# A planned instruction order for two transformer layers: tables that change along the stream, and 3741 operations moved in the queues

## The chip, the cores and the metric

The kernel runs on one core of a Trainium2 chip. The core has five engines, each with an in-order queue of its own: TensorE (PE, matmuls), VectorE (DVE), ScalarE (ACT), GpSimd (POOL) and SyncE (SP, which here only issues DMA transfers). Engines wait for each other through semaphores. The metric is the device time of one execution in microseconds; the time before is the median of three runs, 1028.55 us (1028.09 to 1029.22).

## The reference

Two layers, with the same weights, over one sequence of 2048 rows of 448 numbers in bfloat16. Each layer is an attention block A with 16 heads of 28 and a gated mixing and MLP block B, both behind a layer norm and with a residual:

```python
def _A_ref(x, wqkv, wo):
    qkv = (x @ wqkv).reshape(B, S, 3, H, Dh)  # transposed to q, k, v: B, H, S, Dh
    scores = jnp.einsum("bhqd,bhkd->bhqk", q, k) * (Dh ** -0.5)
    p = _softmax(scores, axis=-1)
    o = jnp.einsum("bhqk,bhkd->bhqd", p, v)
    return o.transpose(0, 2, 1, 3).reshape(B, S, D) @ wo

def _B_ref(x, w1, w2, w3, w4):
    h = _gelu(_layernorm(x, axis=-1) @ w1)
    # four column groups of h, moved by +1, -1, +2 and -2 rows
    x1 = x + jnp.concatenate([g0, g1, g2, g3], axis=-1) @ w2
    return x1 + _gelu(_layernorm(x1, axis=-1) @ w3) @ w4

x = A_x
x = x + _A_ref(_layernorm(x), A_wqkv, A_wo)
x = x + _B_ref(_layernorm(x), B_w1, B_w2, B_w3, B_w4)
x = x + _A_ref(_layernorm(x), A_wqkv, A_wo)
x = x + _B_ref(_layernorm(x), B_w1, B_w2, B_w3, B_w4)
```

Per layer there are 16 x 2048 x 2048 exponentials of scores. They are the largest single piece of work off TensorE.

## The kernel before, in words

**Tiling.** The 2048 rows are 16 tiles of 128. Queries are handled in five chunks a layer (`CHUNKS`: tiles 0-3, 4-7, 8-11, 12-13, 14-15), heads in four groups g of four heads j, keys in tiles of 128. A *block* is one head's scores of 128 keys against 512 queries (or two key tiles against 256), that is one bank of PSUM; there are 2048 of them. `ORDER` says in which order chunks meet which key tiles, so that layer 2 can start while parts of layer 1 are still unfinished; a chunk that is interrupted spills its partial sums through `uscr`.

**The stream of scores.** `t_scores` takes blocks from the list `stream` and writes them into banks 0 to 2 (even unit numbers u) and 3 to 4 (odd ones); `score_ops` issues their matmuls (L1510). `t_exp` then lets ACT take the exponential of a whole unit, two or three blocks, in one instruction into `PT` (L1748). `t_pv` multiplies the results by the values into bank 5 (L1765). A unit waits until the unit two before it has been read out, and its place in `PT` until the product that used it last is done.

**Blocks for DVE.** Some blocks go to DVE instead, which builds the exponential with five instructions: `d_first` reads the bank into `yd` (L1592), `d_chain` does two steps of a polynomial in `fb` (L1619, L1621), scales it into `PD` (L1623) and puts the exponent's bits in (L1626). Which blocks those are is decided while the plan is made, by the tables `R_RATE` (a block takes the third bank of an even unit, which then has two blocks for ACT) and `D_RATE` (a block takes a spare bank), and by limits such as `DTH`, `DDTH`, `DLO`, `DHI` on DVE's load and on how far ahead the block lies.

**Everything else** is written as Python generators that hand in one operation after another and run beside this stream: the layer norms (L1100, L1101, L1106 to L1115), the projections (`proj`, all column-tiled products being issued at L915 as four matmuls of one operation), the norm of the softmax (`t_norm`), the output projection (`t_outproj`), the two halves of block B (`t_mixA`, `t_mixB` with the first product of the MLP evacuated at L2180 by DVE, or at L2176 by ACT with the gelu in it if the exps are all planned; the gelu of a group of tiles in one ACT instruction at L2202) and `t_w4`, its second product. Each ACT switch between exp and gelu costs a table load before and after.

**Two engines for one operation.** The function `both` plans an operation on POOL with DVE as the other choice. Squares of q and k (`sq`) always go to POOL; `z2` (L2019), `xx` (L2105) and `otn` (L1862) go to whichever is free earlier by the plan.

**Fills.** `Sched.keep_pe_busy` puts matmuls of no use (`filler`, L2248, four matmuls of 256 columns into a dead bank) into TensorE's queue wherever the plan leaves it idle, as far as `TARGET` and `WIN` ask.

**The planner.** `Sched.run` simulates the engines with durations written in the generators and picks the next operation by the time at which it could start and by its priority (`RANK` and others). `DOUBT` and `DOUBT2` add margins for results that come from DMA, POOL, DVE or ACT. What comes out is one list of operations (`Plan.all`), numbered in the order in which they were planned, and a queue for each engine. `Plan.add` works out from what an operation reads and writes which others it has to wait for, so any order of the list that keeps the data right is a valid program.

**A rearranged plan.** `Plan.rearranged(moves, weave)` is in the kernel before but unused, since `WEAVE` is empty. For each pair (a, b) of `moves` it takes operation a out of its engine's queue and puts it back right behind operation b. Then it adds all operations anew: `weave` is a string with one letter for each, t, s, v, g or d for PE, ACT, DVE, POOL or SP, and each letter adds the next operation of that engine's queue. At the end it makes sure that every operation reads what the same operations as before have written.

The queues before hold 9619 operations: 6328 of PE, 884 of ACT (781 of them exps), 1587 of DVE, 458 of POOL and 362 of SP. Of PE's, 1171 are fills. 108 blocks are DVE's.

Of the kernel before, what the change touches and what calls it, by code (L numbers as in the profile page):

```python
# [15 lines left out]
ENGS = ("pe", "act", "dve", "pool", "sp")  # L16


MOVES = ()
WEAVE = ()  # L20

FILL_MORE = ()

# [241 lines left out]
class Sched:  # L265
    LAT = {"pe": 0.23, "act": 0.175, "dve": 0.145, "pool": 0.2, "sp": 0.2}
    OWN = {"pe": 0.0, "act": 0.15, "dve": 0.125, "pool": 0.05, "sp": 0.05}
    DOUBT = {"dma": 0.6, "pool": 0.4, "dve": 0.15, "act": 0.1}
    DOUBT2 = {"dma": 0.0, "pool": 0.0, "dve": 0.0, "act": 0.0, "pe": 0.0}
# [354 lines left out]
RLO = 5  # L624
# [45 lines left out]
FMO = 1.59  # L670
SWT = 0.103
Sched.DOUBT = {'dma': 0.8, 'pool': 0.6, 'dve': 0.05, 'act': 0.05}
Sched.LCRED = 0.3


# [4 lines left out]
def build_kernel(nc, A_x, A_wqkv, A_wo, B_x, B_w1, B_w2, B_w3, B_w4, out, n_layers=2):  # L680
# [85 lines left out]
    with st:  # L766
# [864 lines left out]
        def t_scores():  # L1631
# [38 lines left out]

            ringed = set()
            while True:
                if u == 1:
                    yield ("acq", ["b3"])
                    yield ("acq", ["b4"])
# [433 lines left out]
        def t_mixB(L, ch, tiles, direct, pr):  # L2109
# [12 lines left out]
            if direct:  # L2122
                yield from tr_pe(slots, xt)
                for xs in slots:
                    yield ("rel", xs)
            wide = False
            hname = None
            small = L == 0 and tiles == SMALL
            if small:
                yield ("wait", ("kvfree",))  # L2130
                hb = vaug[:, 9:16, :].rearrange("p a b -> p (a b)").rearrange("p (f w) -> p f w", w=NW)
                hkey = [[("vaug", 9 + k) for k in range(f * NW // 512, (f * NW + NW - 1) // 512 + 1)] for f in range(14)]
            elif direct:
                hb, hkey = PT, [[("pt", f)] for f in range(14)]
            else:
                hname = yield ("acq", ["h2T", "h2W"] if ("xdone", 1) in SC.events else ["h2T"], [("xT", xt)])
                wide = hname == "h2W"
                if wide:
                    hkey = [[("vaug", 9 + f)] if f < 7 else [("kT", g, 2 + f) for g in range(4)] for f in range(14)]
                else:  # L2140
                    hb, hkey = h2T, [[("h2T", f), ("xst",)] for f in range(14)]
# [4 lines left out]
                return vaug[:, 9 + f, 128 * i:128 * i + 128] if f < 7 else kT[:, i, 128 * (2 + f):128 * (3 + f)]  # L2146

            late = []
            soft = TANHW.get((L, tiles[0]), 0) and not direct
            fps = 512 // NW  # L2150
            parts = [list(range(f, min(f + fps, 14))) for f in range(0, 14, fps)]
            if wide:
# [89 lines left out]
        def t_final():  # L2242
            for t in range(NT):
                yield ("wait", ("x2", 1, t))
            yield op("sp", 0.05, lambda e: e.nop(), deps=odmas)
# [44 lines left out]
        SC.spawn(t_extra(0, 16), 3)  # L2290
        SC.spawn(t_extra(1, 9), 3)
        SC.spawn(t_final(), 9)
        est = SC.run()

        def again(fn, k):
            return lambda e: [x for _ in range(k) for x in fn(e)]
# [63 lines left out]
```

## Time and profile before

| | |
|---|---|
| median of three runs | 1028.55 us |
| the profiled execution | 1028.86 us |
| its span, first to last instruction | 1027.1 us |
| busy PE / DVE / ACT / POOL | 973.3 / 823.3 / 980.3 / 293.1 us |
| DMA | 62.73 MB, mean 61 GB/s |

A line of the profile names a group by line of the kernel, engine, operation and tiles (out<-in), with the number of instructions; then busy time and the mean length of one; then the time its engine was idle just before them and what ended that. PE's matmuls overlap, so that means of one are longer than their share of the busy time. PEld is the weight load of a matmul. Releasers are inferred.

### The profile page before, as it was taken

How to read it: one execution, taken by the hardware profiler on the slowest of the kernel's cores; microseconds unless marked ns; L12 is line 12 of the kernel's file. 1: busy time of each engine (PE TensorE's matmuls, PEld its weight loads, DVE VectorE, ACT ScalarE, POOL GpSimd, SP SyncE). 2: the span in 40 equal slices, each digit the busy share in tenths (PEclk: the TensorE clock that was granted, in tenths of full speed). 3: DMA queues.
4: the chain of work that ended last, by engine and by line, in shares of the span. 5: the costliest groups of instructions: out<-in, count | busy, mean ns of one | idle time of the engine just before them, and what ended most of it. 6: DMA issues, size and time to landing. Idle time of an engine off the chain costs nothing.

```text
span 1027.1 us, 38497 instructions
## 1 busy us (share of the span) xinstructions
PE 973.3 (95%) x17443; PEld 414.8 (40%) x17445; DVE 823.3 (80%) x1587; ACT 980.3 (95%) x898; POOL 293.1 (29%) x462
## 2 busy tenths in 40 slices
PE   8999999999998999999989999999999999999998
PEld 4332443443333344433343343344433343444465
DVE  7778989998887878778978688788888978887742
ACT  7999999999999999999997999999999999999942
POOL 2322121521435006144335122211535140423120
PEclk9999999999999999999999999999999999999999
DMA  4443341212311002321124017433302020121000
GB/s 120 130 115 105 98 107 50 56 36 53 89 42 33 14 23 61 72 44 37 38 72 77 25 44 174 121 85 92 75 13 38 23 60 27 34 64 37 13 21 25
DMA packets 99404, 62.73 MB, mean 61 GB/s; under 512 B 68712, under 2 KB 88552, under 8 KB 99240
## 3 DMA queue, kind: packets, MB, share of 16 engines
q1 hardware_dynamic: 99240, 60.27, 23.5%
q8 instruction: 136, 2.23, 1.0%
q14 instruction: 28, 0.23, 0.1%
HBM read 28.16 MB, written 16.76 MB: 44 GB/s over the span
## 4 chain that ended last, share of the span: by engine, by line
ACT 83%; PE 13%; DVE 2%; DMA 2%; issue 0%; DVEq 0%; SPq 0%; ACTq 0%
ACT PT L1748 77%; PE ps L915 9%; ACT h2T L2202 2%; PE ps L1510 2%; ACT fb L2021 2%; PE ps L1765 1%; PE ps L2248 1%; ACT L1748 1%; ACT L2202 1%; DMA xT<-xnd 1%; DMA xT<-xn 0%; DMA xnd<-xn 0%; PE ps L1139 0%; ACT vaug L2202 0%; ACT sq L1245 0%
## 5 line engine op out<-in xcount | busy, mean ns | idle before, releaser
L1748 ACT ACTIVATE PT<-ps 128x1024 bf16<-128x1024 f32 (+1 forms) x781 | 885.9, 1406 | 7.4 <-PE ps L1510 7.1
L1510 PE MATMUL ps<-qT,kT 32*128 32x512 bf16 (+1 forms) x2304 | 269.0, 335 | 29.4 <-ACT PT L1748 24.1
L1765 PE MATMUL ps<-PT,vaug 128*32 128x512 bf16 (+1 forms) x2423 | 202.7, 343 | 0.0
L2248 PE MATMUL ps<-ident 128*32 128x256 bf16 x4684 | 173.0, 276 | 1.8 <-POOL ident L1000 1.5
L1510 PEld LDWEIGHTS ps<-qT,kT 32*128 32x128 bf16 x2304 | 69.5, 91 | 257.2 <-ACT PT L1748 249.4
L915 PE MATMUL ps<-xT,w 128*32 128x512 bf16 (+3 forms) x2592 | 158.1, 341 | 3.2 <-DMA xT<-xn 1.5
L2248 PEld LDWEIGHTS ps<-ident 128*32 128x32 bf16 x4684 | 119.3, 98 | 38.8 <-issue 14.7
L1862 POOL TENSOR_TENSOR otn<-ub,fb 128x512 bf16<-128x512 f32 (+1 forms) x32 | 36.9, 1152 | 198.5 <-DMA fb<-rscr 198.4
L1765 PEld LDWEIGHTS ps<-PT,vaug 128*32 128x32 bf16 x2423 | 58.9, 94 | 76.8 <-issue 68.6
L1592 DVE TENSOR_SCALAR yd<-ps 128x512 int32<-128x512 f32 x106 | 72.6, 686 | 17.2 <-PE ps L1510 16.2
L915 PEld LDWEIGHTS ps<-xT,w 128*32 128x32 bf16 (+1 forms) x2592 | 61.6, 95 | 55.3 <-issue 23.9
L1619 DVE SCALAR_TENSOR_TENSOR fb<-yd 128x512 f32<-128x512 uint16 x106 | 78.5, 743 | 0.4
L1621 DVE SCALAR_TENSOR_TENSOR fb<-fb,yd 128x512 f32<-128x512 f32 x106 | 77.1, 728 | 1.0
L1626 DVE SCALAR_TENSOR_TENSOR PD<-yd,PD 128x512 int16<-128x512 int16 x106 | 74.8, 707 | 1.5
L915 PE MATMUL ps<-w,h2T 128*32 128x448 bf16 x1120 | 67.8, 354 | 1.0 <-ACT h2T L2202 0.6
L2180 DVE CAST h2T<-ps 128x512 bf16<-128x512 f32 (+1 forms) x70 | 44.5, 636 | 19.0 <-PE ps L915 18.3
L1248 POOL TENSOR_TENSOR sq<-kT 128x512 bf16<-128x512 bf16 (+2 forms) x32 | 31.1, 976 | 78.7 <-DVE kT L1262 61.3
L1248 POOL TENSOR_TENSOR sq<-qT 128x512 bf16<-128x512 bf16 x24 | 27.0, 1128 | 79.2 <-DVE qT L1307 73.9
L1623 DVE TENSOR_SCALAR PD<-fb 128x512 bf16<-128x512 f32 x107 | 46.8, 438 | 1.7
L1510 PE MATMUL ps<-wk_pad,kT 32*128 32x512 bf16 x256 | 37.8, 384 | 4.9 <-ACT PT L1748 4.0
L2019 POOL TENSOR_TENSOR fb<-hT 112x512 f32<-112x512 bf16 (+1 forms) x21 | 23.8, 1133 | 63.3 <-DVE hT L1991 25.6
L1765 PE MATMUL ps<-PD,vaug 128*32 128x512 bf16 (+1 forms) x136 | 40.7, 339 | 0.0
(195 smaller groups left out, 1215.1 us busy)
## 6 DMA issues: line engine op xcount, KB each, us to landing
uscr<-ub SPq DMA_DIRECT2D x28, 256.0 KB
ub<-uscr SPq DMA_DIRECT2D x28, 256.0 KB
fb<-rscr SPq DMA_DIRECT2D x24, 256.0 KB
xnd<-xn SPq DMA_DIRECT2D x28, 128.0 KB, 3.0
xd<-x_res SPq DMA_DIRECT2D x16, 224.0 KB, 3.4
x_res<-xd SPq DMA_DIRECT2D x16, 224.0 KB, 3.5
w<-in_B_w_dram SPq DMA_DIRECT2D x5, 448.0 KB, 8.8
obf<-in_A_x_dram SPq DMA_DIRECT2D x16, 112.0 KB, 2.8
```

What stands on the lines that cost most here:

```text
L915: r.append(e.matmul(out=out[c:c + w, :], lhsT=lhsT[:, c:c + w], rhs=rhs, start=start, stop=stop, tile_position=(0, c)))
L1248: return both("sq", 0.15 + NW * 0.0018, 0.07 + NW * 0.00104, lambda e: e.tensor_tensor(out=sq[:, si, 0:NW], in0=src, in1=src, op=ALU.mult) ...
L1510: yield op("pe", (0.005 + NW * 0.00042) / nc_, lambda e, i=i, kc=kc, j=j, g=g, qt=qt, a=a, NW=NW, bank=bank: e.matmul(out=ps[:, bank, i * ...
L1592: yield op("dve", c_ps(512), lambda e: e.tensor_scalar(out=y, in0=ps[:, bi(bank), :], scalar1=SCALE * L2E * FS, scalar2=-126.0 * FS, op0=A ...
L1619: yield op(D_[0][0], D_[0][1], lambda e: e.scalar_tensor_tensor(out=q, in0=lo, scalar=E2 / E3 * FS, in1=lo, op0=ALU.add, op1=ALU.mult), re ...
L1621: yield op(D_[1][0], D_[1][1], lambda e: e.scalar_tensor_tensor(out=q, in0=q, scalar=E1 / E3 * FS * FS, in1=lo, op0=ALU.add, op1=ALU.mult) ...
L1623: yield op(D_[2][0], D_[2][1], lambda e: e.tensor_scalar(out=pdt, in0=q, scalar1=E3 / FS ** 3, scalar2=E0, op0=ALU.mult, op1=ALU.add), rea ...
L1626: yield op(D_[3][0], D_[3][1], lambda e: e.scalar_tensor_tensor(out=pdt.bitcast(I16), in0=hi, scalar=128.0, in1=pdt.bitcast(I16), op0=ALU. ...
L1748: yield op("act", EXPC + n * w * 0.000833, lambda e, bk=bk, s0=s0, n=n, w=w: e.activation(out=PT[:, s0:s0 + n, 0:w], in_=ps[:, bk[0]:bk[0] ...
L1765: r.append(e.matmul(out=ps[32 * j:32 * j + 32, 5, 0:NW], lhsT=vaug[:, vs, 32 * (4 * g + j):32 * (4 * g + j) + 32], rhs=buf[:, s, i * NW:(i ...
L2180: ev = op("dve", c_ps(m * NW), lambda e, hr=hr, pv=pv: e.tensor_copy(out=hr, in_=pv), reads=[("ps", bi(b))], writes=hk, touch=[b])
L2248: return [e.matmul(out=ps[32 * c:32 * c + 32, bi(b), 0:256].rearrange("p (a n) -> p a n", n=128), lhsT=ident[:, 32 * c:32 * c + 32], rhs=i ...
```

## The change

Three things. First, a table `TWEAK` sets planner parameters anew at 40 unit numbers u of the score stream: `tweak(TWEAK.get(u, ()))` is called at the head of each round of `t_scores`. The parameters are those of `KNOBS` and of the planner itself; the values hold until they are set again. `knobs()` keeps the old ones and puts them back after planning. The first entry acts at u = 6. Second, in `t_mixB` the flag `soft` is worked out earlier, and a group that is soft no longer takes the wide buffer `h2W`. Third, `MOVES` gets 3741 pairs and `WEAVE` a string of 9450 letters, so that the plan goes through `Plan.rearranged`.

```diff
-MOVES = ()
-WEAVE = ()
+MOVES = (
+    (109, 69), (110, 109), (111, 110), (112, 111), (72, 86), (70, 72), (75, 70), (77, 75), (113, 77), (74, 113), (104, 74), (76, 104), (73, 76),
+    (93, 73), (102, 93), (91, 102), (71, 90), (100, 92), (99, 100), (98, 99), (96, 98), (87, 95), (119, 115), (120, 116), (127, 131), (147, 153),
...
+    (8423, 8476), (8033, 8423), (9020, 8711), (8381, 9020), (8257, 8989),
+)
+WEAVE = (
+    'vdvvdvvvsdgvvgdgvtvtgtdvtgtttdgttvttttdvttvvttvdtttttvvtdvtttttdtvvvgvdgsvdvsgvdgsvttdsvtttdsvtvtttdtttgtvstttttvtttgvstvstttttvvttttstvvtvtsvtvgtstvt'
...
+    'tttvstvttgtvtdtgtvtttgsvtttdttgttsdtttttgtttttvttdsttstvttstvttsttttvttttttttvtttttvttttttvtttttvtttttvtttttvtvttsgttgttgtttttgststtgvtsgtsgvtttgttttgtttgtt'
+    'tgtvttvtttvsttttdttttttttstttttttstttttststttttttttvtttvttttvvttttgttvtttttvtttvtvtgtgttvtgtgttttgvttgvttgttgttttttvtstvtsttvtdttvtgtttttttttdtvttgvtt'
+    'vtvtttgtdtttttttttttttttttttttttttttttvttttvtttstdttstdtstttsttstttttsttttttttsttstttsttsttstttttsttttsttsttttttttttttttttvtttdttttttttttttttvtttdtvdd'
+)
...
+KNOBS = ("RANK", "R_RATE", "D_RATE", "Q_LEAD", "PE_NORM", "TANHW", "W_POS", "DPRIO", "UPRIO", "DWIN", "DTH", "DDTH", "RLO", "RHI", "DLO", "DHI", "DURG", "FMD", "FMO")
+TWEAK = {6: [('RANK', ('w', 1, 0), 1.401), ('D_RATE', 6, 0.105), ('RANK', ('m', 0, 3), 2.499), ('D_RATE', 1, 0.276), ('R_RATE', 0, 0.168), ('R_RATE', 1, 0.057), ('RANK', ('n', 0, 0), 0.821)],
...
+def tweak(items):
+    for (name, key, val) in items:
+        if name.startswith("Sched."):
+            if key is None:
+                setattr(Sched, name[6:], val)
+            else:
+                getattr(Sched, name[6:])[key] = val
+        elif key is None:
+            globals()[name] = val
+        else:
+            globals()[name][key] = val
+
+
+def knobs():
+    keep = {k: globals()[k] for k in KNOBS}
+    for k, v in keep.items():
+        if isinstance(v, dict):
+            globals()[k] = dict(v)
+    sch = {k: getattr(Sched, k) for k in ("TARGET", "WIN", "LWIN", "EARLY", "LCRED", "LOW", "AGED", "DOUBT", "DOUBT2")}
...
+    def back():
+        globals().update(keep)
+        for k, v in sch.items():
+            setattr(Sched, k, v)
+    return back
...
             while True:
+                tweak(TWEAK.get(u, ()))
                 if u == 1:
...
+            soft = TANHW.get((L, tiles[0]), 0) and not direct
             wide = False
...
-                hname = yield ("acq", ["h2T", "h2W"] if ("xdone", 1) in SC.events else ["h2T"], [("xT", xt)])
+                hname = yield ("acq", ["h2T", "h2W"] if ("xdone", 1) in SC.events and not soft else ["h2T"], [("xT", xt)])
...
-            soft = TANHW.get((L, tiles[0]), 0) and not direct
...
+        back = knobs()
         est = SC.run()
+        back()
```

Counted letter by letter, the new string has 6198 t, 884 s, 1557 v, 449 g and 362 d. In the head, both lists number the operations alike: 54 to 69, 78 to 86 and 109 to 115 are fills; 70 to 77 the transposes of the first two row tiles; 87, 95, 96, 98, 99, 100, 102 and 104 those of the next two; 90 to 93 small sums of squared weights. Letters are in the order in which operations are added, which follows their time only roughly.

More of the change, by code (lines that the diff above doesn't have):

```diff
@@ new lines, in tweak @@
+def tweak(items):
[16 more added lines that the diff above has]
+    for k, v in sch.items():
+        if isinstance(v, dict):
+            setattr(Sched, k, dict(v))
+    def back():
+        globals().update(keep)
+        for k, v in sch.items():
+            setattr(Sched, k, v)
+    return back
```

61 lines of the change are left out of this document (added), and 365 rows, old and new, of the table MOVES.

## The prediction

> **What bounds the kernel now.** First the page's engine totals and the engine shares of the chain that ended last.
>
> ```profile
> PE 973.3 (95%) x17443; PEld 414.8 (40%) x17445; DVE 823.3 (80%) x1587; ACT 980.3 (95%) x898; POOL 293.1 (29%) x462
> ACT 83%; PE 13%; DVE 2%; DMA 2%; issue 0%; DVEq 0%; SPq 0%; ACTq 0%
> ```
>
> PE and ACT look equally full, but the chain is 83% ACT. The windows (busy time per stretch, in the order PE, PEld, DVE, ACT, POOL) show why.
>
> ```profile
> 100.00:200.00 100.00, 95.19 (x1814) 42.85 (x1806) 89.74 (x176) 100.00 (x92) 24.20 (x36) 1.00 0.32 83
> 200.00:300.00 100.00, 94.71 (x1609) 37.95 (x1609) 90.48 (x161) 99.92 (x89) 31.07 (x49) 1.00 0.23 57
> 500.00:600.00 100.00, 93.36 (x1618) 39.24 (x1618) 76.59 (x149) 93.78 (x86) 34.13 (x49) 1.00 0.23 55
> 950.00:1000.00 50.00, 48.65 (x1034) 28.37 (x1038) 30.29 (x65) 35.68 (x41) 8.74 (x23) 1.00 0.07 17
> 1000.00:1027.00 27.00, 23.85 (x532) 13.88 (x520) 8.20 (x14) 7.68 (x16) 2.53 (x4) 1.00 0.08 24
> ```
>
> ACT is idle for nothing from 100 to 300, loses 6.2 us in 500 to 600, and is done early: in the last 77 us PE is busy 72.5. So there are three stages: a head to the first exp, a stream of exps on ACT, a tail on PE. The timeline of ACT gives their edges and the wait in the middle.
>
> ```profile
> 17.06 2.38 ACT L1748 ACTIVATE PT<-ps 128x1536 bf16<-128x1536 f32 x2
> 540.53 1.05 ACT L1748 ACTIVATE PT<-ps 128x1024 bf16<-128x1024 f32 x1
> 547.41 1.45 ACT L1748 ACTIVATE PT<-ps 128x1536 bf16<-128x1536 f32 x1 [5.83 <-PE ps L1510]
> 967.13 5.74 ACT L1748 ACTIVATE PT<-ps 128x1536 bf16<-128x1536 f32 x5
> ACT PT L1748 <- PE ps L1510: 7.1, 4, 5.8
> ```
>
> Head 17.06, stream 955.8 (to 972.87), tail 54.2. Of the stream's waits for scores, 7.1 us in all (the last row, from the waits), 5.83 are one wait. Nothing that reorders queues shortens the stream by more than about 7 us; beyond that only fewer or cheaper ACT operations do. PE before the exps has room, as the group of score weight loads shows:
>
> ```profile
> L1510 PEld LDWEIGHTS ps<-qT,kT 32*128 32x128 bf16 x2304 | 69.5, 91 | 257.2 <-ACT PT L1748 249.4 <-issue 4.7 <-ACT fb L2021 1.2
> ```
>
> 249.4 us of waiting for banks over 781 exps is 0.32 us each: a disturbance of PE below that is absorbed, a larger one reaches ACT.
>
> **The change, part by part.** The new order string has one letter for each operation, so it can be counted against the queues before: TensorE 6198 (before 6328), ACT 884 (884), DVE 1557 (1587), POOL 449 (458), SP 362 (362). From this each part follows.
>
> *Work of ACT.* On POOL only three kinds of operation have a second form on DVE (z2, xx, otn), so POOL's 9 go to DVE. DVE then has 39 fewer of its own. A block of scores on DVE is 5 operations; the rest is evacuations that ACT takes if they are planned after the last exp. Behind the last exp the old queues hold 31 ACT operations, the new string 26. I choose the split that meets both counts, 6 evacuations back on DVE and one gelu more (31 - 6 + 1 = 26), for then 39 = 5 x 9 - 6: 9 blocks fewer on DVE, 99 in place of 108, and, ACT's total being equal, 5 exps more (786). The prices:
>
> ```profile
> L1748 ACT ACTIVATE PT<-ps 128x1536 bf16<-128x1536 f32 x378 | 614.1, 1625 | 6.5 <-PE ps L1510 6.4
> L1748 ACT ACTIVATE PT<-ps 128x1024 bf16<-128x1024 f32 x403 | 477.8, 1201 | 0.8 <-PE ps L1510 0.8
> 950.74 1.34 ACT PT L1748
> 958.12 2.26 ACT PT L1748 x2
> ```
>
> The means overlap, so I take the chain: a three-block exp 1.34, one of each 2.26, hence 0.92 for two, 0.42 a block and 0.08 fixed. 9 x 0.42 + 5 x 0.08 = **+4.2 us** of ACT in a stream that has no room. With 8 or 10 blocks it is 3.8 to 4.6.
>
> *Work of DVE.* Nine blocks, at the five means below, free 9 x 3.30 = 29.7 us; nine POOL operations cost at most 9 x 0.79, six evacuations about 6 x 0.69, by the first row, which reads from PSUM too.
>
> ```profile
> L1592 DVE TENSOR_SCALAR yd<-ps 128x512 int32<-128x512 f32 x106 | 72.6, 686 | 17.2 <-PE ps L1510 16.2
> L1619 DVE SCALAR_TENSOR_TENSOR fb<-yd 128x512 f32<-128x512 uint16 x106 | 78.5, 743 | 0.4
> L1621 DVE SCALAR_TENSOR_TENSOR fb<-fb,yd 128x512 f32<-128x512 f32 x106 | 77.1, 728 | 1.0
> L1626 DVE SCALAR_TENSOR_TENSOR PD<-yd,PD 128x512 int16<-128x512 int16 x106 | 74.8, 707 | 1.5
> L1623 DVE TENSOR_SCALAR PD<-fb 128x512 bf16<-128x512 f32 x107 | 46.8, 438 | 1.7
> L2105 DVE TENSOR_TENSOR x_res<-x_res,x1b 128x448 f32<-128x448 f32 x5 | 4.0, 790 | 0.2
> ```
>
> DVE is 18 us emptier and not the bound: nothing. But it isn't even: up to ACT operation 440 the new string has 18 DVE letters more than the old queues, by 560 it has 12 fewer. Cover is ACT's stream; without it the 18 x 0.7 = 13 us land on a DVE that is 90% busy from 100 to 300.
>
> *Fills.* All TensorE work but the fills (L2248) is fixed, so the 130 are fills.
>
> ```profile
> L2248 PE MATMUL ps<-ident 128*32 128x256 bf16 x4684 | 173.0, 276 | 1.8 <-POOL ident L1000 1.5
> ```
>
> 4684 matmuls in 173.0 us, four a fill: 0.148 each, 19 us of PE time, all in the stream behind ACT: nothing. The opposite end is a lower clock, a rival below.
>
> *The middle wait.* At 541 the order on PE is this:
>
> ```profile
> 541.36 1.88 PE L915 MATMUL ps<-w,h2T 128*32 128x448 bf16 x36
> 543.07 1.95 PE L915 MATMUL ps<-xT,wq_pad 128*32 128x512 bf16 x32
> 545.57 0.40 PE L915 MATMUL ps<-sq,astatq 128*32 128x512 bf16 x4 [0.56 <-DVE qT L1307]
> 545.90 0.38 PE L1510 MATMUL ps<-qT,kT 32*128 32x512 bf16 x1
> 518.31 4.23 DMA xT<-xn
> ```
>
> The first scores of layer 2 stand behind their own queries, and these behind 36 matmuls of the MLP's second product. In the old queues ACT operations 464 and 479 have 41 and 35 TensorE operations between them and their predecessor: a long gelu, and this wait. In the new string the gelu is at 438 with 48, and up to 547 no other has more than 11. I read that as the queries done in time: **-5.8 us**. Least: 0, when the wait only moves; most: -7.1, all waits.
>
> *The tail.* The chain gives PE's pace there.
>
> ```profile
> 976.98 6.67 PE ps L915 x172
> 984.21 19.76 PE ps L915 x500
> 1005.53 18.34 PE ps L915 x416
> ```
>
> That is 39, 40 and 44 ns a matmul, 0.16 to 0.18 an operation of four. Behind the last exp the old queues hold 319 TensorE operations, the new string 291 (the last 36 + 255 letters). 28 fewer are **-4.7 us**, moved under ACT's stream in place of fills. Least: 0, if the chain through DVE and POOL is what ends last; most: -9.2, if the 77.0 - 72.5 = 4.5 us that PE idles in the last two windows go too.
>
> *The head.* Up to the seventh exp both plans are the same, so the first moves can be read by number: 70 to 77 are the transposes of the first two tiles, 78 to 86 and 109 to 115 fills.
>
> ```profile
> 1.52 3.61 PE L2248 MATMUL ps<-ident 128*32 128x256 bf16 x64 [1.52 <-POOL ident L1000]
> 7.21 2.11 PE L2248 MATMUL ps<-ident 128*32 128x256 bf16 x36
> 9.48 0.91 PE L1139 MATMUL ps<-ident,xn 128*128 128x128 bf16 x7
> 10.32 1.12 PE L2248 MATMUL ps<-ident 128*32 128x256 bf16 x28
> 10.00 0.85 DVE L1146 COPY xT<-ps 128x512 bf16<-128x512 bf16 x2 [1.52 <-PE ps L1139]
> ```
>
> Now nine fills (36 matmuls) stand between the two halves of the transposes, and DVE waits 1.52 us for the second. Afterwards 29 fills come first (16, four of the later ones, and the nine), then all transposes mixed. At 3.61 / 16 = 0.226 a fill they end at 1.52 + 29 x 0.226 = 8.1; sixteen transposes at 0.91 / 7 take 2.1: 10.2, against 10.39 now. But the first tile's copy then waits too: its last transpose is the tenth in the new order, 8.1 + 10 x 0.13 = 9.4. I take **-0.3**, between -1.1 (the later fills no longer ahead of the projections) and +1.0 (four copies in a row).
>
> **Sum.** 4.2 - 5.8 - 4.7 - 0.3 = -6.6 us. The profiled execution took 1028.86 us with a span of 1027.1 (1.8 around it), near the median of 1028.55. 1028.86 - 6.6 = **1022.3 us**. Its own terms reach from 1028.86 + 3.8 - 7.1 - 9.2 - 1.1 = 1015.3 to 1028.86 + 4.6 + 0 + 0 + 1.0 = 1034.5, the upper end being also where a rival lies.
>
> **Rivals.** *A wait for another engine stands ahead of scores (slower).* Place: PE's queue between 500 and 620, where the layers meet. Up to ACT operation 560 the new string has issued 224 transfers where the old queues had 236, and 3741 operations stand where the planner's margins for late DMA and DVE no longer hold. PE works in order: an operation that waits there, say, for xT (4.23 us of DMA in the chain above) keeps all scores behind it. Beyond 0.32 us each microsecond reaches ACT. One stall as long as today's 5.83 gives 1028.1; it decides from 6.6 us on, and two give 1022.3 + 11.7 = **1034**. For it: the 12 transfers. Against: by 640 the counts are equal (279 and 278), and no long run of TensorE letters stands there.
>
> *The clock.* The first 64 fill matmuls take 56 ns each, the 28 from 10.32 on 40, the average 37: PE is slower early, though the windows grant 1.00 everywhere. With real work at (973.3 - 173.0) / 1027.1 = 78% of the span, PE at such a pace (56 / 37 = 1.5 times) needs 1.17 of the time and ACT loses 0.17 us each; 80 us of it would cost 14: 1036. Against: 130 of 1171 fills is a ninth, and PE stays above 90%.
> [...]
>
> *The wait only moves.* The queries of layer 2 hang on that layer's normalised tiles and on free buffers, not on order alone; then the middle term is 0: 1028.1, no change.
>
> *More falls out.* Fewer fills may mean a plan that is shorter as a whole: 130 fills at 0.11 us in the plan's own price are 14.3 us, which gives **1014**. Against: exps are not fewer, and only 7 us of stream waits exist, so it needs a tail of 46 us.
>
> **Chances.** Forecast 0.50 (own range 1017 to 1026.5); more 0.17; wait moved, no change 0.10; stalls 0.18; clock 0.05. A measurement here tells 0.2% (2 us) from nothing, so faster is 0.67, same 0.10, slower 0.23. The range is 1012 to 1034.5: it leaves out half of the stalls and the clock, and the far end of "more", and takes in the bounds of the terms.
>
> **What would show it.** Exps: 786, about 377 of them with 1536 columns (2048 blocks less 99, less 2 x 786), and 99 blocks in the five DVE groups; then the 4.2 is right. ACT's wait for scores: below 2 us in all; a wait above 3 us between 500 and 620 is the stall or the moved wait. Tail: from the last exp's end to the end 49.5 us; first exp near 16.8. L2248 near 4164 matmuls, clock 1.00. The forecast is wrong if ACT idles for more than 10 us between its first and last exp, or if the last exp ends after 975.

## The result, and the profile after

| | before | after |
|---|---|---|
| median | 1028.63 us (4 runs) | 1046.19 us (4 runs, 1044.62 to 1051.66) |
| ratio to before | | 1.0176, interval 1.0153 to 1.0199 |
| the profiled execution | 1028.86 us | 1047.29 us |
| its span | 1027.1 us | 1045.2 us |
| first exp to end of the last | 955.8 us | 975.3 us |
| tail behind it | 54.2 us | 52.8 us |

The change made the kernel 1.8% slower. The forecast was 1022.3 us, its range ended at 1034.5, and the chance given to slower was 0.23. In the kernel after, the exps are at L2216 (before L1748), the scores at L1977 (L1510), the column-tiled products at L1382 (L915), the product with the values at L2233 (L1765), the fills at L2716 (L2248) and the first DVE operation of a block at L2059 (L1592).

The page of the kernel after has these engine totals and this chain:

```profile
PE 980.3 (94%) x16925; PEld 413.4 (40%) x16925; DVE 807.1 (77%) x1557; ACT 991.0 (95%) x898; POOL 282.2 (27%) x453
ACT 45%; PE 38%; DVE 12%; DMA 3%; POOL 1%; issue 1%; SPq 0%; DVEq 0%; ACTq 0%
```

The busy shares look as before. The chain doesn't: ACT held 83% of it and now holds 45%, because it leaves ACT again and again for PE, and from there for DVE and DMA. The timeline of ACT gives the edges of the stream:

```profile
17.01 1.44 ACT L2216 ACTIVATE PT<-ps 128x1536 bf16<-128x1536 f32 x1
979.98 12.38 ACT L2216 ACTIVATE PT<-ps 128x1536 bf16<-128x1536 f32 x11
```

The last exp ends at 992.36, where before it ended at 972.87. Head and tail are nearly what they were, so the 18.1 us of span are lost between the exps. The windows (busy PE, PEld, DVE, ACT, POOL, then the granted clock) show how:

```profile
100.00:200.00 100.00, 93.24 (x1701) 41.09 (x1704) 88.06 (x177) 98.65 (x89) 20.81 (x25) 1.00 0.23 63
200.00:300.00 100.00, 95.62 (x1573) 38.18 (x1565) 88.35 (x160) 99.12 (x89) 24.14 (x46) 1.00 0.20 45
500.00:600.00 100.00, 93.51 (x1543) 37.50 (x1539) 76.54 (x146) 98.36 (x89) 39.68 (x63) 1.00 0.20 49
```

The one long wait of before in 500 to 600 is gone (ACT 93.78 before, 98.36 now), but in 100 to 200, where ACT had been busy for all 100 us, it now idles 1.35 us. Idle time is the smaller part of the loss. The groups by shape show the other:

```profile
L2216 ACT ACTIVATE PT<-ps 128x1536 bf16<-128x1536 f32 x386 | 575.6, 1491 | 10.8 <-PE ps L1977 9.6
L2216 ACT ACTIVATE PT<-ps 128x1024 bf16<-128x1024 f32 x395 | 420.3, 1067 | 3.2 <-PE ps L1977 2.4
L2059 DVE TENSOR_SCALAR yd<-ps 128x512 int32<-128x512 f32 x97 | 66.4, 686 | 31.8 <-PE ps L1977 29.7
L2716 PE MATMUL ps<-ident 128*32 128x256 bf16 x4164 | 156.4, 277 | 5.2 <-POOL ident L1467 2.3
```

A single exp is shorter than before (1491 for 1625 ns, 1067 for 1201). That isn't a faster ACT. An exp that has its scores in time starts before the end of the one ahead of it, by 0.30 us before and 0.14 after, and its record is longer by that (1.64 and 1.21 us with three and two blocks before, 1.48 and 1.06 after); one that comes late starts 0.01 us behind that end, is shorter, and the overlap is lost (medians over the traces). What an exp adds to ACT's stream is the same in both kernels, by the median over the trace: 1.343 us with three blocks, 0.916 with two. A late exp takes 1.45 and 1.02 (medians), also in both, so that coming late costs about 0.11 us even where ACT shows no gap. I call an exp *late* if it ends more than 20 ns later than that allows, gaps ahead of it included. Before there are 17 late exps and they cost 9.1 us (5.83 of it the wait at 541); after there are 107, which cost 23.3 us. Of these, 91 are late by less than 0.32 us and cost 9.9 together; the other 16 cost 13.4. ACT's wait for scores, which the prediction saw at below 2 us in all, is

```profile
ACT PT L2216 <- PE ps L1977: 12.0, 18, 2.2
```

The stream's 19.5 us are then: eight more three-block exps in place of two-block ones (386 for 378), 8 x 0.427 = 3.4; late exps 23.3 - 9.1 = 14.2; 1.9 are left. As much lies in the 39 operations on `fb` that ACT does for the gated mixing (L2489, before L2021): they add 17.4 us to ACT's stream before and 19.3 after, where four of them wait for DVE, 1.2 us together.

Where the slack went is in the source view of the scores' line: what ended the idle time of PE or of its weight load just before a score matmul or its load, in us and times. First before, then after:

```profile
  ACT PT L1748: 314.8, 827
  issue: 4.7, 16
```

```profile
  ACT PT L2216: 231.2, 580
  issue: 90.2, 299
```

"ACT PT" means that the scores had come up in the queue and waited for a bank that ACT was still reading: PE was ahead. "issue" means that they waited for nothing; the bank had long been free, and PE came late to it. 16 times before, 299 times after.

### The profile page after: what moved, and what is told of

It is laid out like the page before. It is cut to its first block, busy times and chain, and to the rows that moved or that the text cites. A ratio compares the mean times of both kernels' runs of the same rounds, so it can differ in the third digit from the quotient of the medians.

```text
span 1045.2 us, 37446 instructions
## 1 busy us (share of the span) xinstructions
PE 980.3 (94%) x16925; PEld 413.4 (40%) x16925; DVE 807.1 (77%) x1557; ACT 991.0 (95%) x898; POOL 282.2 (27%) x453
## 4 chain that ended last, share of the span: by engine, by line
ACT 45%; PE 38%; DVE 12%; DMA 3%; POOL 1%; issue 1%; SPq 0%; DVEq 0%; ACTq 0%
ACT PT L2216 43%; PE ps L1382 18%; PE ps L1977 10%; PE ps L2716 5%; PE ps L2233 5%; DVE fb L2088 1%; DVE fb L2488 1%; DVE PD L2093 1%; DVE st L1567 1%; DVE fb L2086 1%; DVE yd L2059 1%; ACT fb L2489 1%; DMA xT<-xnd 1%; DVE qT L1774 1%; DVE PD L2090 1%
## 5 line engine op out<-in xcount | busy, mean ns | idle before, releaser
L2216 ACT ACTIVATE PT<-ps 128x1024 bf16<-128x1024 f32 (+1 forms) x781 | 894.0, 1277 | 14.0 <-PE ps L1977 12.0
L1977 PE MATMUL ps<-qT,kT 32*128 32x512 bf16 (+1 forms) x2304 | 294.6, 336 | 28.9 <-ACT PT L2216 25.5
L2233 PE MATMUL ps<-PT,vaug 128*32 128x512 bf16 (+1 forms) x2432 | 182.2, 344 | 1.7 <-ACT PT L2216 0.7
L1977 PEld LDWEIGHTS ps<-qT,kT 32*128 32x128 bf16 x2304 | 77.1, 91 | 264.1 <-ACT PT L2216 174.4
L2716 PE MATMUL ps<-ident 128*32 128x256 bf16 x4164 | 156.4, 277 | 5.2 <-POOL ident L1467 2.3
L1382 PE MATMUL ps<-xT,w 128*32 128x512 bf16 (+4 forms) x2656 | 155.7, 344 | 4.8 <-DVE h2T L2648 2.3
L2716 PEld LDWEIGHTS ps<-ident 128*32 128x32 bf16 x4164 | 99.8, 97 | 50.7 <-issue 25.8
L2059 DVE TENSOR_SCALAR yd<-ps 128x512 int32<-128x512 f32 x97 | 66.4, 686 | 31.8 <-PE ps L1977 29.7
L1382 PEld LDWEIGHTS ps<-xT,w 128*32 128x32 bf16 (+1 forms) x2656 | 59.7, 95 | 62.0 <-issue 24.0
L2233 PEld LDWEIGHTS ps<-PT,vaug 128*32 128x32 bf16 x2432 | 57.2, 95 | 66.8 <-issue 44.1
L2086 DVE SCALAR_TENSOR_TENSOR fb<-yd 128x512 f32<-128x512 uint16 x97 | 68.1, 705 | 1.5
L2330 POOL TENSOR_TENSOR otn<-ub,fb 128x512 bf16<-128x512 f32 (+1 forms) x23 | 28.2, 1226 | 148.3 <-DMA fb<-rscr 147.9
L1382 PE MATMUL ps<-w,h2T 128*32 128x448 bf16 x1008 | 60.4, 354 | 0.2 <-DVE x_res L2686 0.2
L1573 POOL TENSOR_SCALAR vpe<-mv 128x1 f32<-128x1 f32 (+2 forms) x21 | 7.8, 373 | 145.9 <-DVE mv L1568 145.9
L1977 PE MATMUL ps<-wk_pad,kT 32*128 32x512 bf16 x256 | 41.7, 384 | 5.5 <-ACT PT L2216 4.8
L1382 PE MATMUL ps<-xT,wk_pad 128*32 128x512 bf16 (+2 forms) x512 | 34.6, 366 | 3.8 <-issue 1.7
```

Of the source, the lines that this page charges most:

```text
L1382: r.append(e.matmul(out=out[c:c + w, :], lhsT=lhsT[:, c:c + w], rhs=rhs, start=start, stop=stop, tile_position=(0, c)))
L1977: yield op("pe", (0.005 + NW * 0.00042) / nc_, lambda e, i=i, kc=kc, j=j, g=g, qt=qt, a=a, NW=NW, bank=bank: e.matmul(out=ps[:, bank, i * ...
L2059: yield op("dve", c_ps(512), lambda e: e.tensor_scalar(out=y, in0=ps[:, bi(bank), :], scalar1=SCALE * L2E * FS, scalar2=-126.0 * FS, op0=A ...
L2086: yield op(D_[0][0], D_[0][1], lambda e: e.scalar_tensor_tensor(out=q, in0=lo, scalar=E2 / E3 * FS, in1=lo, op0=ALU.add, op1=ALU.mult), re ...
L2216: yield op("act", EXPC + n * w * 0.000833, lambda e, bk=bk, s0=s0, n=n, w=w: e.activation(out=PT[:, s0:s0 + n, 0:w], in_=ps[:, bk[0]:bk[0] ...
L2233: r.append(e.matmul(out=ps[32 * j:32 * j + 32, 5, 0:NW], lhsT=vaug[:, vs, 32 * (4 * g + j):32 * (4 * g + j) + 32], rhs=buf[:, s, i * NW:(i ...
```

## The experiments

All ran against the kernel before. "Late" is counted as above; "stream" is from the first exp to the end of the last in the profiled execution.

### The tables without the moves

```diff
-MOVES = (
-    (109, 69), (110, 109), (111, 110), (112, 111), (72, 86), (70, 72), (75, 70), (77, 75), (113, 77), (74, 113), (104, 74), (76, 104), (73, 76),
...
+MOVES = ()
...
+WEAVE = ()
```

> The new tables alone: the queues stand as the planner leaves them with them, MOVES and WEAVE empty. Theory Q (the edited queues lose the time, the tables are good): 1020 to 1028 us, exps wait for scores below 8 us in the stream, last exp over by 972. Rival T (the tables' plan itself is the loss, by its smaller margins for DMA or its fewer fills): 1040 us or more, waits and a lower clock as in the changed kernel.

1025.86 us (7 runs, 1024.05 to 1027.07); ratio 0.9968, interval 0.9956 to 0.9979. Stream 955.3, tail 53.0, late exps 21 costing 5.7 us. Waits of ACT for scores and the source view of the scores' line:

```profile
ACT PT L1783 <- PE ps L1544: 3.6, 5, 1.5
```

```profile
  ACT PT L1783: 345.4, 858
  issue: 7.0, 24
```

The tables alone are a gain of some 3 us. The wait of 5.83 us is gone, and PE is ahead of ACT as it was before. The 3741 moves, which the prediction priced at next to nothing, cost some 20 us. The remaining runs ask how.

### Fills where the clock fell

The granted clock of the kernel after isn't 1.00 throughout. Timeline rows of PE and of ACT, and windows around them:

```profile
412.24 1.40 PE L1382 MATMUL ps<-xT,wk_pad 128*32 128x512 bf16 x12 [1.71 <-DMA xT<-xnd]
656.67 0.83 PE L1382 MATMUL ps<-xT,wk_pad 128*32 128x384 bf16 x16 [1.75 <-issue]
924.31 1.17 PE L1382 MATMUL ps<-w,hT 112*32 112x448 bf16 x8 [0.83 <-DVE obf L2701]
```

```profile
414.23 1.45 ACT L2216 ACTIVATE PT<-ps 128x1536 bf16<-128x1536 f32 x1 [2.22 <-PE ps L1977]
```

```profile
410.00:415.00 5.00, 3.29 (x46) 0.99 (x38) 2.04 (x5) 2.78 (x3) 0.00 (x0) 0.74 0.82 128
655.00:660.00 5.00, 3.33 (x45) 1.08 (x45) 4.08 (x7) 3.69 (x4) 0.94 (x1) 0.81 0.73 216
925.00:930.00 5.00, 5.00 (x76) 1.70 (x76) 3.96 (x10) 3.28 (x3) 0.79 (x2) 0.72 0.19 62
```

Three times PE stood before a product that had to wait, with scores behind it in its queue: for transfers into `xT` at 412 and 656 (there the view names no releaser, but the last piece of such a transfer landed at 656.58), for DVE at 924. Each time the clock was halved for 3.4 us afterwards, and ACT then lost 1.2 to 2.2 us at once. The late exps at the three places cost 7.8 us together. So fills were put ahead of those three products.

```diff
-FILL_MORE = ()
+FILL_MORE = ((3673, 11), (5919, 11), (8425, 6))
```

(and three pairs in `MOVES` that set these fills ahead of the three products)

> The changed kernel with 25 fills more, 11, 11 and 6 repeats of one fill put ahead of the three TensorE operations before which it idles and the clock falls to half (near 411, 655 and 923 us). Theory C (the lower clock is itself a part of the loss): the clock stays at 1.00 and the time falls by 5 to 8 us, to 1038 to 1041. Rival: the late operand is the loss and the clock only follows it: 1045 to 1047.

1044.4 us (4 runs, 1044.04 to 1048.12); ratio 1.0161, interval 1.0141 to 1.0181. In the profiled execution the clock is 1.00 at the three places, and halved at two others, 464.3 and 815.9. Late exps 103, 20.8 us; of the 106 units that are late by over 0.02 us in the change's profile, 92 are late here too, 80 of them by the same time within 0.03 us. So the lateness belongs to the order and not to the execution. The time lies between the two ranges that were expected, next to the one in which the late operand is the loss. What the clock alone costs this run doesn't tell: the halving only moved, and the medians of change and run, 1.8 us apart, differ less than the runs of either. Among the change's own four runs, the two with a mean clock of 0.997 took 1044.62 and 1045.1 us, those with 0.995 and 0.992 1047.29 and 1051.66.

### Two attempts on the scores

`MOVES` and `WEAVE` were made anew twice. First the change's order, but with no scores later than the planned order has them, up to number 8500 (2804 pairs); then the planned order, with only the scores, and a dozen fills bound to them, where the change has them (1874 pairs).

```diff
-    (147, 153), (114, 164), (170, 167), (173, 168), (179, 173), (177, 179), (190, 184), (196, 207),
+    (147, 153), (114, 164), (179, 173), (177, 179), (201, 190), (193, 207), (197, 193), (200, 197),
...
```

```diff
-    (109, 69), (110, 109), (111, 110), (112, 111), (72, 86), (70, 72),
+    (82, 127), (83, 82), (84, 83), (85, 84), (109, 85), (110, 109),
...
```

> The changed kernel, but every score matmul stands no later in TensorE's queue than where the planner had it (counted by the other TensorE operations ahead of it); all other moves stay, up to plan number 8500. If the small delays of about a hundred exps come from other work put ahead of scores: 8 to 15 us faster than the changed kernel, 1031 to 1038. If they come from results that are late whatever stands where, or from the clock: within 3 us of 1046.

> The tables' own queues with only the score matmuls (and 12 fills bound to them) at the depth at which the change has them; all else as planned. If the place of the scores is the loss: 1038 to 1046. If it is the moves of the other work: like the tables alone, within 3 us.

1072.3 us (ratio 1.0426, 1.0392 to 1.046) and 1126.03 us (1.096, 1.0915 to 1.1006): far outside what either theory said. Waits of ACT in the first and in the second:

```profile
ACT PT L2082 <- PE ps L1843: 32.0, 47, 2.9
```

```profile
ACT PT L2005 <- PE ps L1766: 83.8, 106, 5.1
```

Scores put elsewhere among the other work of PE, all else staying, are worse than both orders they are mixed from. These runs don't tell the theories apart.

### PE's moves, and the others' moves

```diff
-    (109, 69), (110, 109), (111, 110), (112, 111), (72, 86), (70, 72),
+    (776, 780), (1849, 1855), (3865, 3881), (3908, 3905), (5476, 5473),
...
```

The first kernel keeps PE's queue as planned (1172 pairs are left), the second moves only PE's (2607 pairs).

> The new tables and all moves of the change on VectorE, ScalarE, GpSimd and SyncE, but TensorE's queue as the planner left it (51 overtakes and 102 places differ from it, because the moved operations of the other engines demand it). The tables alone took 1025.86 us, the change 1046.19. If the 20 us are TensorE's moves (scores behind other products and behind products whose operands are late): 1024 to 1031, with ACT waiting for scores under 5 us and the stream's late exps costing under 8 us. If they are the moves of VectorE and the queues, which make TensorE's operands late: 1038 to 1046. If it is the two orders being made apart (as in the two mixed orders before): above 1050, with late exps of 50 us or more.

> The reverse: the new tables, TensorE's queue moved as in the change, the queues of the other engines as the planner left them (22 overtakes; on VectorE 30 and on ScalarE 6 places differ). If the 20 us are TensorE's moves: 1040 to 1048, the late exps costing some 20 us as in the change. If they are the other engines' moves: 1024 to 1031. If any mixture of two orders loses: above 1050.

1188.95 us (ratio 1.1542, 1.1517 to 1.1567) and 1152.93 us (1.1206, 1.1162 to 1.125). The third case of both expectations: the change's orders on PE and on the other engines fit each other, and neither can be taken away alone. So the 20 us can't be given to one engine in this way.

### The moves cut in time

At number 5000 (planned for about 527 us) the two orders can be joined on all five queues at once, without any operation out of its place.

```diff
...
-    (4992, 4986), (4993, 4992), (5008, 5003), (5012, 5008), (5006, 5012), (5014, 5019),
+    (4992, 4986), (4993, 4992), (4997, 4990),
...
```

```diff
-    (109, 69), (110, 109), (111, 110), (112, 111), (72, 86), (70, 72),
+    (5008, 5003), (5012, 5008), (5006, 5012), (5014, 5019), (5013, 5014),
...
```

> The new tables; the moves of all five queues only for the operations up to the plan's number 5000 (planned for about 527 us), the rest as planned: 1946 operations moved. The tables alone take 1025.9, the change 1046.2. If the loss is spread with the moves: about 1036 (1033 to 1039), late exps of 10 to 15 us up to 530 us and as few as with the tables alone behind it. If it sits in one half, or comes from the joint of the two orders: 1026 to 1029 or 1043 to 1047; above 1050 if any mixture of the two orders loses.

> The other half: planned queues up to number 5000, the moves behind it (1795 operations). If the loss is spread: about 1036 (1033 to 1039), few late exps up to 530 us and 10 us or more behind it, and the gains of the two halves and the tables add up to the change's 17.6 us within 3. If it sits in one half: 1026 to 1029 or 1043 to 1047.

1036.14 us (ratio 1.0086, 1.0061 to 1.0112) and 1038.33 us (1.0096, 1.0062 to 1.013). Each half costs about half. By the ratios, the tables' -3.3, +12.1 and +13.2 give +22.0 where the change has +18.1: 3.9 more, which is over the 3 that were expected, with intervals of some 3 us on each term. The profiled executions agree better: the streams are 7.0 and 13.9 us longer than the tables' 955.3, together 20.9 where the change's is 20.0. Late exps cost 12.1 and 17.7 us, and they lie where the moves are: 11.2 of 12.1 before 600 us in the first, 15.5 of 17.7 after 600 in the second. The windows of the first and of the second show it on ACT:

```profile
200.00:300.00 100.00, 94.90 (x1550) 37.78 (x1546) 88.11 (x160) 98.90 (x88) 25.13 (x47) 1.00 0.19 45
700.00:800.00 100.00, 94.35 (x1670) 38.84 (x1658) 83.65 (x152) 100.00 (x92) 34.39 (x65) 1.00 0.26 60
```

```profile
200.00:300.00 100.00, 94.16 (x1581) 37.32 (x1579) 89.70 (x164) 99.94 (x91) 27.47 (x47) 1.00 0.20 53
700.00:800.00 100.00, 94.84 (x1631) 39.68 (x1631) 80.28 (x146) 99.33 (x90) 30.99 (x51) 1.00 0.23 56
```

So do the scores that came up late, in the source views of the first and of the second half:

```profile
  issue: 51.3, 174
```

```profile
  issue: 48.8, 159
```

24 with the tables alone, 174 and 159 with a half, 299 with all. The loss is spread with the moves; it isn't one place where the layers meet.

The clock has a part in the second half. In the first half's profiled execution it is never halved; in the second's it is, at 644.7, 914.3 and 958.7, for 17.1 us, and 9.8 of the 17.7 us of late exps lie there (from 1.5 us ahead of such a stretch to 3 us behind it). Away from halved clocks late exps cost 2.6 us with the tables, 12.1 and 7.9 with the halves and 15.5 with the change: these add up within 2 us. Near them they cost 3.1, 0, 9.8 and 7.8, the waits that came ahead of the halving included. Two runs of the second half, with mean clocks of 0.997 and 0.998, took 1036.28 and 1034.54 us, the other two, with 0.992 and 0.990, 1040.38 and 1041.31; that may be why the ratios don't add up.

### The late scores set earlier

If a unit is late because the wrong products stand ahead of its scores, setting just those scores earlier should help (3747 pairs in place of 3741).

```diff
-    (195, 196), (193, 195), (197, 193), (200, 197), (206, 209), (215, 211), (232, 227), (230, 228),
+    (195, 196), (193, 195), (197, 211), (200, 197), (206, 200), (215, 206), (232, 227), (230, 228),
...
```

> The change, with the scores of 100 of the 106 units whose exp came late in its profile set 0.1 to 0.7 us earlier in TensorE's queue (227 places in all, 0.36 us on average by the plan's durations); all else as in the change. 92 of those units are late again, by the same amount, in the other profile of the change's order (with more fills), so the lateness sits in the order. If it comes from what stands directly ahead of each late unit's scores: the late exps fall from 23.3 us to under 10, and the time to 1030 to 1037. If TensorE is behind as a whole there (the products ahead only change places, and the next unit is late instead): 1043 to 1050, with as many late exps as before.

1049.28 us (ratio 1.0212, 1.0194 to 1.0229). Of the 106 units (the 107 without the first exp of all), 30 are still late, and what the 106 cost went from 23.2 us to 8.9. But 66 others are late now and cost 14.2, 59 of these within three units of one that was late before. The sum, 23.2 us, has not moved. One case in the timelines of ACT, first the change and then this kernel:

```profile
526.67 1.02 ACT L2216 ACTIVATE PT<-ps 128x1024 bf16<-128x1024 f32 x1 [0.81 <-PE ps L1977]
527.59 0.62 ACT L2489 ACTIVATE fb<-fb 128x512 f32<-128x512 f32 x1
528.52 3.71 ACT L2216 ACTIVATE PT<-ps 128x1536 bf16<-128x1536 f32 x3 [0.31 <-PE ps L1977]
```

```profile
525.83 2.45 ACT L2161 ACTIVATE PT<-ps 128x1536 bf16<-128x1536 f32 x2 [0.71 <-PE ps L1922]
528.57 1.45 ACT L2161 ACTIVATE PT<-ps 128x1536 bf16<-128x1536 f32 x1 [0.29 <-PE ps L1922]
```

In the change unit 411 is 0.81 us late. Its scores stand behind this product, which waits for DVE:

```profile
525.91 0.40 PE L1382 MATMUL ps<-kT,w 128*32 128x256 bf16 x8 [1.32 <-DVE vaug L2641]
526.24 0.39 PE L1977 MATMUL ps<-qT,kT 32*128 32x512 bf16 x2
```

Set earlier, unit 411 is in time; 412 is then 0.71 late and 414 is 0.29. PE is behind as a whole there, and this order, too, hands the delay to the next.

### Room on PE

The opposite: no operation changes its place, but PE gets time.

```diff
+        def little(e, b):
+            return [e.matmul(out=ps[0:32, bi(b), 0:32], lhsT=ident[:, 0:32], rhs=ident[:, 0:32], start=True, stop=True, tile_position=(0, 0))]
+
...
+        for i in FILL_LESS:
+            args = P.args[i]
+            assert args[0] == "pe" and args[2] == [("ident",)]
+            P.args[i] = (args[0], lambda e, b=args[3][0][1]: little(e, "b%d" % b)) + args[2:]
```

> The change's order, place for place. Of its 1041 fills, the 346 that stand within the last 2 us of TensorE's planned work ahead of the scores of the 106 late units are cut from four matmuls of 256 columns to one of 32 (by the plan 38 us of TensorE's time; 47 of the 106 units have at least their lateness in fills ahead of them). If the late exps come from too little room in TensorE's time there, and not from which product stands next to which: the late exps fall from 23.3 us to 10 to 15, and the time to 1034 to 1039, if the clock stays at 1.00 in most slices. If room is not what lacks: 1043 to 1048. If TensorE then idles enough for the clock to halve in many places: above 1050.

> The same with all 1009 fills between 20 and 955 us of the plan cut to one matmul of 32 columns (some 108 us of TensorE's time by the plan). If fills do nothing but take room: late exps under 15 us, time 1030 to 1038. If they hold the clock: the granted clock under 0.97 and the time above 1060.

1043.32 us (1040.1 to 1053.48; ratio 1.0157, 1.0105 to 1.0209) and 1070.99 us (1.0414, 1.0397 to 1.0432). The first profiled execution is the slowest of its four; its clock is halved 10 times, for 58 us together, where the change's was three times. By its median the run falls into the range expected if room is not what lacks, 1043 to 1048. The clock decides here: the four runs, with mean clocks of 0.992, 0.989, 0.984 and 0.972, took 1040.1, 1042.59, 1044.05 and 1053.48 us, and a straight line through them gives, as an estimate, 1035 at 1.00, in the range expected for room. The profiled execution, divided in the same way as the halves, agrees: 89 of the late units lie away from halved clocks. In the change they cost 18.4 us; here they cost 7.4, and units that weren't late before add 0.7. Near the halved clock the late exps cost 21.4 us. So room does cure the lateness, by some 10 us, and the clock takes it back: without these fills the four runs have mean clocks of 0.972 to 0.992, where the change's have 0.992 to 0.997. This division was made after the run, and no run has the room without the lower clock. With all fills cut this is plain in the windows:

```profile
100.00:200.00 100.00, 84.97 (x867) 27.48 (x871) 83.55 (x166) 93.47 (x84) 18.39 (x22) 0.76 0.21 58
500.00:600.00 100.00, 92.07 (x1444) 35.18 (x1444) 76.62 (x142) 98.34 (x92) 36.16 (x57) 1.00 0.21 50
```

Clock 0.76 in the stretch that has most fills, 0.906 over the execution, halved for 201.4 us. Away from the halved clock late exps cost 6.9 us, near it 40.0. The theory that fills do nothing but take room is out.

### The tables with one fill more

The tables alone had one place of their own where the clock was halved, behind this wait (timeline of PE, and the window behind it):

```profile
404.86 0.40 PE L949 MATMUL ps<-xT,wk_pad 128*32 128x512 bf16 x4 [1.83 <-DMA xT<-xnd]
```

```profile
405.00:410.00 5.00, 5.00 (x72) 1.57 (x64) 3.47 (x7) 2.49 (x3) 3.64 (x4) 0.66 0.39 83
```

```diff
+MOVES = (
+    (3673, 3680),
+)
-FILL_MORE = ()
+FILL_MORE = ((3673, 11),)
```

(with a `WEAVE` that otherwise keeps the order as planned)

> The tables alone, and one fill moved ahead of the column-tiled product that waited 1.83 us for its xT transfer at 404.9, repeated 11 times, so that TensorE has work there. The tables alone took 1025.86 us and showed one halving of the clock at 406.3, whose late exps cost some 3 us. If the idle of TensorE brings the halving: none there, and 1022.5 to 1024. If the clock is not tied to that wait, or the halving moves to another place: 1025 to 1027.

1025.07 us (6 runs, 1024.08 to 1027.15); ratio 0.9965, interval 0.9952 to 0.9978. The same window:

```profile
405.00:410.00 5.00, 4.96 (x92) 1.79 (x88) 2.85 (x4) 4.80 (x5) 4.09 (x9) 1.00 0.62 63
```

In the profiled execution the halving is gone, nowhere else has one come, and the stream is 953.6, 1.7 us shorter. But two of the six runs have a mean clock below 1.00, 0.998 and 0.997, and they are the slowest, 1026.12 and 1027.15 us. The medians of the two kernels can't be told apart, and the time lies in the range, 1025 to 1027, expected if the clock isn't tied to that wait. Both versions beat the kernel before, by 0.3%, and the change.

## Why the prediction was wrong

**The step that failed** is the first conclusion from the weight loads of the scores: 249.4 us of waiting for banks over 781 exps "is 0.32 us each: a disturbance of PE below that is absorbed". From it followed that the moves had no price of their own outside the head. The 249.4 us were real, but they were a sum of what the old order had left in each place, and a new order doesn't inherit them. With the moves, 299 score loads find their bank already free, where it was 16; 107 exps are late in place of 17, most of them (91) by less than 0.32 us. The mean slack of an order says nothing about what another order leaves.

**What the moves did**, as far as the runs show it. PE is busy 94% of the span, so a delay there is made up for slowly, and ACT's two groups of banks let PE be one unit ahead and no more. With the moves PE waits more in its own queue for operands of other engines: the rows of its waits in the stream, all but those for ACT's exps, sum to 11.6 us in 22 waits before, to 10.8 in 16 with the tables, to 20.4 in 42 with the moves, and to 13.2 in 27 and 17.4 in 35 with half of them. Here are the first rows behind those for ACT, of the change:

```profile
PE ps L1382 <- DVE h2T L2648: 2.5, 4, 1.3
PE ps L1382 <- issue: 1.7, 1, 1.7
PE ps L1382 <- DMA xT<-xnd: 1.7, 1, 1.7
PE ps L1382 <- DVE vaug L2641: 1.3, 1, 1.3
```

Each such wait takes PE's lead away, and the exps behind it come late while PE itself is busy: in front of 99 of the 107 late exps PE was idle for less than 0.3 us of the 1.6 us before (as it was in front of 88% of the others). That it is PE's time which lacks there is supported from both sides: given room, the same units fell from 18.4 to 7.4 us, away from halved clocks; reordered, they only handed the delay on (23.2 us of late exps before and after). What isn't shown is how much of the 20 us is these waits and how much an uneven spread of PE's work. The plan's own durations speak for some of the second (units whose scores end 1.3 to 1.5 us of PE work after those of the unit ahead: 8 by the tables' plan, 47 by the change's order), but only 12 of those 47 are late, for 1.0 of the 23.3 us. Nor is it shown which pairs do the harm, since the orders of the engines couldn't be taken apart.

**The rival** "a wait for another engine stands ahead of scores" named a mechanism that is at work, and with 0.18 gave it too small a chance. Its place (500 to 620, the layers' meeting) and its size (one or two stalls as long as the old one) were wrong: the largest single wait of ACT was 2.22 us, at 412, behind an `xT` from DMA, and late exps lie all along, 16 above 0.32 us and 91 below.

**The clock** rival (0.05, an even slowdown of PE by fewer fills) did not come. With as many fewer fills, the tables alone run at 0.998 and gain. Short halvings behind PE's waits are some of the loss: 7.8 us of the change's late exps lie at its three, 3.1 of the tables' at their one. How much of that is the clock's own and how much the waits' isn't shown.

**The terms of the sum**, against the tables alone, which are the change without its moves:

- *ACT's work, +4.2.* Measured 3.4. The blocks of DVE fell by 8, not 9 (2048 - 386 x 3 - 395 x 2 = 100), and the exps stayed 781, because the units were not more in number but eight of them wider. The letters count an engine's operations, not their kinds, and I chose one split that fitted; the prices, 1.34 and 0.92, were right to 0.01. One of the two counts that the split had to meet was misread: behind the last exp the rearranged list holds 30 ACT operations, not 26.
- *DVE and fills, nothing.* Right with the tables alone: 100 blocks, 4164 fill matmuls as counted, and no loss. DVE was no bound.
- *The middle wait, -5.8.* The wait itself is gone: no wait of ACT for scores above 1.5 us is left with the tables, and in the change none between 530 and 560. But late exps as a whole fell only from 9.1 to 5.7 us with the tables, by 3.5, since others are late now, 3.1 us of them at the halved clock.
- *The tail, -4.7.* Measured -1.2 with the tables, -1.4 in the change. The price was right: PE is busy there for all of the first 49.13 us before, and for 49.14 of 49.64 in the change, at 43 ns a matmul. The count was wrong: after the end of the last exp the traces have 1178 matmuls before, 1166 with the tables and 1154 in the change, 3 and 6 operations of four fewer instead of 28. I had taken the 36 letters of PE ahead of the 859th of ACT for the end of the exps. Followed through the queues, the last exp is ACT's 854th operation, and 311 operations of PE stand behind it in the list: 8 fewer than the 319 before, not 28. With the tables alone it is 315.
- *The head, -0.3.* Measured -0.05, 17.06 to 17.01, and not to be told from nothing: with the head as planned the first exp came at 16.98 with the tables alone and at 16.19 with one fill more.

With the measured sizes of the tables the sum is 3.4 - 3.5 - 1.2 = -1.3 us, and the profiled executions differ by 1.8. By the ratio of all runs the tables gain 3.3; their profiled execution was the slowest of seven. So the tables bring about half of the 6.6 us that were forecast for the whole, and that is in part luck: the two large gains, 5.8 and 4.7, measured 3.5 and 1.2. The moves, the larger part of the text of the change, had no loss of their own in the sum at all. The prediction's own sign for being wrong, a last exp that ends after 975, is what came: 992.36.

## What to carry to other kernels

Where an engine paces the end and another feeds it at 94% busy, as here, an order is a balance in each short stretch, not only a set of dependencies; price a reordering as an unknown with a loss in every stretch that it touches, and don't cover it with the mean slack of the old order. Count how often the feeder found its buffer already free: that number (16 here, 299 after) tells a lost lead before any long wait shows. When several things change together, run each alone before explaining the sum: here a gain of 3 us was hidden under a loss of 20. And look at the clock of each run before giving a cause its price: runs of one kernel that differ in it lie up to 13 us apart here.

## What the hardware did that I had not expected

I had not expected the clock to be halved after pauses as short as these. A wait of PE of 0.83 to 1.83 us, with PE busy again at once, was followed by one period of 3.4 us at half clock: at 412 (PE busy 3.29 of 5 us), 656 (3.33 of 5) and 924 in the change, and at 406 with the tables. Not every such pause did it: unit 411's wait of 1.32 us at 525 left the clock at 1.00 (525 to 530, PE busy 4.09 of 5 us). The prediction had priced the clock as an even slowdown only.

The traces show a little more. In the change each halved period lasts 3.41 us, and they begin at 412.37, 658.12 and 924.36, the second and third 72 and 150 times 3.41 us behind the first. The starts given above for two other runs, 464.3 and 815.9 with more fills and 644.7, 914.3 and 958.7 with the second half, also lie whole multiples of that apart, within their rounding (103, 79 and 13). In the step of 3.41 us just ahead of them PE was busy for 50, 49 and 70% of the time in the change, with the tables for 46%; in the step that holds most of unit 411's wait, 525.00 to 528.41, it was busy for 73%. From these five steps I read, as an estimate, that the halving goes with how busy PE was over such a step and not with one pause alone. No sharp limit shows: in the change there is also a step at 69%, 84.69 to 88.10, that no halving followed.

The fills therefore stand on both sides. With the 346 fills ahead of late units cut, PE in 195 to 205 us was busy 9.36 of 10 us, and the granted clock was 0.66 all the same, where the change has 9.39 and 1.00:

```profile
195.00:205.00 10.00, 9.36 (x127) 3.69 (x127) 8.85 (x16) 8.74 (x9) 2.67 (x6) 0.66 0.23 48
```

At half clock PE counts as busy, too (3.42 of 3.42 us at 0.50 in the change, 412.36 to 415.78), so a high share of busy PE doesn't show that the clock is held; only the clock's own column does.
